# Sigmoid attention and a balanced mixture of experts on one core: quarter-row gathers turned on VectorE for the last two experts, unread products ahead of the first, later places for the routing

## The chip, the core and the metric

The kernel runs on one core of one Trainium2 chip. The metric is device microseconds of one execution; less is better. The engines are TensorE (PE; PEld are its weight loads), VectorE (DVE), ScalarE (ACT), GpSimd (POOL) and SyncE (SP), each with a queue of its own that is worked off in order. DMAs are issued from the queues of SP and POOL.

## What is computed

Inputs: q, k, v of 8 batches, 12 heads, 448 tokens, 64 values each; a gate of 768 x 8; w1 of 8 experts x 768 x 1024, w2 of 8 x 1024 x 768; all float32.

```python
scores = scale * np.matmul(q, k.transpose(0, 1, 3, 2)) - np.log(S)
attn = 1.0 / (1.0 + np.exp(-scores))
x = np.matmul(attn, v)            # then rows of tokens: 3584 x 768
logits = x @ w_gate
order = np.argsort(-logits.flatten())
for idx in order:                 # best pair of token and expert first
    tok, e = (int(idx) // E, int(idx) % E)
    if assigned[tok] >= 0 or counts[e] >= cap:   # cap = 3584 / 8 = 448
        continue
    assigned[tok] = e
    counts[e] += 1
for e in range(E):
    mask = assigned == e
    out[mask] = np.maximum(x[mask] @ w1[e], 0.0) @ w2[e]
```

## The kernel before

**Attention** (lines 484 to 636) runs over 48 pairs of heads and writes the rows x to a DRAM tensor `xs`. The last rows are turned and stored beside the first routing search, up to some 310 us.

**Routing** (`Router.phase`, line 410) finds the experts in eight phases, in the order in which they fill. A phase makes keys (`keys`), turns them on TensorE (line 236), searches a threshold digit by digit on VectorE (`search`; line 281 sets up the digits after the first, line 292 makes the result `kap`), turns that (line 299), and marks the tokens (`pick`, whose last step on VectorE is the column scan of line 326). Then come the *place* (two products, lines 333 and 334), the one-hot tile `r_oh` (line 352), 32 list products (line 360), a copy `r_bt` (line 377), and two products (line 381) that give `r_idx`, the 448 row numbers as four columns of 128. Phase 7 needs no search: `left` takes what remains.

**Experts** (`moe`, line 791) follow one after another, in the program's order, kx = 0 to 7. The first stage has four groups of 36 products per half of w1, 144 x 448 columns in all; after each group ScalarE writes the rectified result as `hb` and `hr` (rounded) and as `h0` (whole; two buffers), and GpSimd writes the remainders from `h0` (line 827). The second stage has two halves of 88 products, 384 columns wide; ScalarE copies the results to `yr` (lines 771 to 783), GpSimd adds one piece (line 784) and scatters the rows to `out` by indirect DMAs (line 757). PSUM has two buffers `sc` for both stages.

**Weights** come in units of 128 x 768, 16 to an expert (8 of w1, 8 of w2, numbered through: expert kx has units 16 kx to 16 kx + 15). A unit is loaded three units ahead (`load_w`) and split two units ahead (`split_w`): ScalarE casts it to `wh`, GpSimd or VectorE subtracts and gives `wl` (line 711). `W_DVE` says which engine: VectorE for units 0 and 1 and for the odd ones from 96.

**Tokens** of the next expert are gathered by four indirect DMAs of whole rows (`gather`, line 731; 128 x 768) and turned in four blocks on TensorE (`xturn`, line 745: two times three transposes a block), from PSUM to `xh` on ScalarE and `xl` on VectorE.

**The order** is written out by hand: `moe` yields after each product with its planned cost (189 or 164 ns), and the driver (line 885) adds these to a clock. When the clock passes `t_route`, the next piece of the routing is emitted, and the T_ numbers set the distance to the piece after; due `chores` (gathers, turning, scatters) are emitted one in 1000 ns, and `flush` empties those that belong to an expert at its end. So the numbers decide where an instruction stands in its queue, and nothing is timed on the chip itself.

Of the kernel before, what the change touches and what calls it, by code (L numbers as in the profile page):

```python
# [54 lines left out]
def route_consts(nc, cp, K):  # L55
# [65 lines left out]
class Router:  # L121
# [217 lines left out]
        nc.vector.tensor_scalar(sl, p[:112, 64:96], BIG, None, OP.add)  # L339
        self.sl = sl  # L340

    def lists(self, alone):

        nc, K, wk, sl = self.nc, self.K, self.wk, self.sl
        P = self.bank()[:112]
# [64 lines left out]
    def phase(self, k):  # L410
        if k:
            self.remove()
        if k < 7:
            if k:
                yield T_KEY
                yield from self.keys()
            yield T_KT if k else T_KEYS
            yield from self.search(k == 0)
            yield T_KAP
            self.pick()  # L420
        else:
            self.left()
        yield T_PICK
        self.place(k == 0)
        yield from self.lists(k == 0)


def moe_attention(tc, q, k, v, w_gate, w1, w2, out):
# [7 lines left out]
    with contextlib.ExitStack() as ctx:  # L436
# [214 lines left out]
        picked, listed = {}, {}  # L651

        def routing():
            for kx in range(E):
                for t in R.phase(kx):
                    if kx not in picked and R.ei is not None:
                        picked[kx] = R.ei
                    yield t
                listed[kx] = R.idx
                R.ei = None  # L660
                yield 0

# [23 lines left out]
        def load_w(u, behind=False):  # L686


            kx, st, i, j = units[u]
            if kx not in gate:  # L690
                gate[kx] = nc.sync.value_load(picked[kx][:1, :1], min_val=0, max_val=E - 1)
            t = wp.tile([128, 768], F32, name="wr")
            if behind:
                nc.gpsimd.memset(t[:1, :1], 0.0)
            if st == 0:
                t = t.rearrange("p (a f) -> p a f", a=3)
                src = w1[ds(gate[kx], 1)].rearrange("e (a p) f -> p (e a) f", p=128)
                nc.sync.dma_start(t, src[:, 3 * j:3 * j + 3, i * 256:(i + 1) * 256])
# [35 lines left out]
        def xturn(kx, j, n, hf, wide):  # L734
# [131 lines left out]
            stream(-1, 2, -1)  # L866
        for j, n in blocks():
            gather(0, j, n)
        stream(-1, 2, 2)
        stream(-1, 4, 2, True)  # L870
        for _ in range(4):
# [13 lines left out]
        for kx in range(E):  # L885
            turned = kx + 1 == E
            start = clock[0]

            def prepare():
                t0 = clock[0]  # L890
                lag = max(5000, min(14000, start + 40000 - t0))
                space = max(TURN_FIRST, min(TURN_NS, (start + EXPERT_NS - t0 - lag - 1000) // 4))
                for j, n in blocks():
                    if kx < 2:
# [4 lines left out]
                def turn_block(j, n):  # L899
# [16 lines left out]
            for step, cost in enumerate(moe(kx)):  # L916
# [12 lines left out]
                    turned = True  # L929
                if turned and kx + 2 in listed and kx + 2 not in fetched:  # L930
                    fetched.add(kx + 2)
                    for j, n in blocks():
                        chores.append((t + 1500 * j, kx + 1, lambda j=j, n=n, e=kx + 2: gather(e, j, n)))
# [39 lines left out]
```

## Time and profile before

| | |
|---|---|
| median of 3 runs | 857.68 us (857.0 to 857.93) |
| profiled execution | 857.27 us, span 855.5 us |
| TensorE busy | 817.9 us, 96% of the span |
| VectorE, ScalarE, GpSimd busy | 538.9, 437.9, 484.4 us |
| attention and first rows | to about 309 us |
| first expert's first product to last product | 325 to 843 us |

The page gives each engine's busy time, the waits say for how long an engine stood idle ahead of an instruction and what ended that, and the timeline lists instructions by their start.

### The profile page before, as it was taken

Reading aid. Unit: us, or ns where it says so; the run is one execution under the profiler, and the core shown is the slowest. Engines: PE = TensorE matmul, PEld = TensorE weight load, DVE = VectorE, ACT = ScalarE, POOL = GpSimd, SP = SyncE. Lnnn points to the kernel's source line nnn. Section 1 sums busy time; section 2 is a strip of 40 time slices with the busy share of each in tenths; the row PEclk is TensorE's granted clock in tenths of the full one; section 3 lists DMA queues with packets and bytes.
Section 4 is the critical chain, followed back from the end, with each engine's and each line's share of the span. In section 5 each row is a group of like instructions: output and inputs, shape, how many; then the busy total and the mean of one; then the engine's idle time right before and its main releaser. Section 6 shows DMA issues by size and latency. Waiting matters only on the chain.

```text
span 855.5 us, 16407 instructions
## 1 busy us (share of the span) xinstructions
PE 817.9 (96%) x5517; PEld 650.2 (76%) x5517; DVE 538.9 (63%) x2069; ACT 437.9 (51%) x603; POOL 484.4 (57%) x506
## 2 busy tenths in 40 slices
PE   6999999999999839999999999999999999999997
PEld 3455455454554728999988999999999989999996
DVE  4565555565554989977978969969879852321211
ACT  6777777778775833425424434434434424443332
POOL 9545444445410014867866866876875885743753
PEclk9999999999999978999999999999999999999999
DMA  9776666656530975345435353453553554443331
GB/s 177 153 153 128 131 129 130 124 118 138 121 65 2 318 254 158 111 138 175 114 106 170 115 147 131 147 169 101 157 166 103 156 156 161 139 129 112 129 103 64
DMA packets 196532, 117.58 MB, mean 137 GB/s; under 512 B 145248, under 2 KB 186208, under 8 KB 196448
## 3 DMA queue, kind: packets, MB, share of 16 engines
q1 hardware_dynamic: 183840, 83.30, 37.6%
q0 software_dynamic: 10752, 33.02, 12.6%
q8 instruction: 43, 0.70, 0.4%
q10 hardware_dynamic: 1856, 0.23, 0.2%
q14 instruction: 41, 0.34, 0.1%
HBM read 94.47 MB, written 22.02 MB: 136 GB/s over the span
## 4 chain that ended last, share of the span: by engine, by line
PE 85%; DVE 10%; issue 2%; DMA 1%; ACT 0%; POOL 0%; ACTq 0%; POOLq 0%; SPq 0%; DVEq 0%
PE sc L856 26%; PE tp L559 13%; PE sc L535 12%; PE sc L811 8%; PE sc L815 8%; PE sc L813 8%; DVE r_junk L178 4%; PE tp L565 3%; PE tp L745 2%; PE sc L545 2%; PE tp L580 1%; PE rt L360 1%; DVE r_j L272 1%; DVE r_T L281 1%; DMA xr<-xs,r_idx 1%
## 5 line engine op out<-in xcount | busy, mean ns | idle before, releaser
L711 POOL TENSOR_TENSOR wl<-wr,wh 128x768 fp32r<-128x768 f32 x110 | 202.3, 1855 | 28.3 <-ACT wh L709 28.0
L856 PE MATMUL sc<-wh,hb 128*128 128x384 f32 x768 | 199.8, 338 | 0.0
L525 ACT ACTIVATE at<-sc,bias 128x896 f32<-128x896 f32 x168 | 160.8, 1004 | 62.2 <-PE sc L545 37.8
L466 POOL DMA_DIRECT2D nkq<-in_q_dram x188 | 118.2, 640 | 114.5 <-DVE kqT L510 109.3
L813 PE MATMUL sc<-xl,wh 128*128 128x448 f32 (+2 forms) x396 | 144.2, 364 | 0.0
L811 PE MATMUL sc<-xh,wh 128*128 128x448 f32 (+2 forms) x396 | 144.2, 364 | 0.0
L815 PE MATMUL sc<-xh,wl 128*128 128x448 f32 (+2 forms) x396 | 143.9, 363 | 0.0
L856 PEld LDWEIGHTS sc<-wh,hb 128*128 128x128 f32 x768 | 138.3, 188 | 1.7 <-issue 0.6
L856 PE MATMUL sc<-wl,hb 128*128 128x384 f32 x384 | 130.8, 341 | 0.0
L709 ACT ACTIVATE wh<-wr 128x768 fp32r<-128x768 f32 x128 | 104.0, 850 | 50.9 <-PE sc L856 29.9
L178 DVE TENSOR_SCALAR_CACHE_REDUCE r_junk<-r_KE,r_T 128x224 bf16<-128x224 f32 x315 | 123.3, 442 | 0.1
L559 PE MATMUL tp<-at,nv 128*64 128x448 f32 x576 | 118.6, 548 | 0.0
L821 ACT ACTIVATE hb<-sc 128x768 fp32r<-128x768 f32 x32 | 26.0, 813 | 134.0 <-PE sc L815 134.0
L519 DVE TENSOR_TENSOR kqL<-kqT,kqH 128x896 fp32r<-128x896 f32 (+1 forms) x49 | 52.5, 1072 | 57.8 <-ACT kqH L517 57.7
L827 POOL TENSOR_TENSOR hb<-h,hb 128x768 fp32r<-128x768 f32 x32 | 59.1, 1848 | 50.4 <-ACT h L824 50.4
L559 PEld LDWEIGHTS tp<-at,nv 128*64 128x64 f32 x576 | 37.1, 136 | 59.4 <-issue 57.1
L813 PEld LDWEIGHTS sc<-xl,wh 128*128 128x128 f32 x396 | 74.6, 188 | 6.9 <-DVE xl L749 0.2
L815 PEld LDWEIGHTS sc<-xh,wl 128*128 128x128 f32 x396 | 74.6, 188 | 6.8 <-issue 0.2
L811 PEld LDWEIGHTS sc<-xh,wh 128*128 128x128 f32 x396 | 74.6, 188 | 6.6
L711 DVE TENSOR_TENSOR wl<-wr,wh 128x768 fp32r<-128x768 f32 x18 | 24.0, 1332 | 82.1 <-ACT wh L709 82.0
L856 PEld LDWEIGHTS sc<-wl,hb 128*128 128x128 f32 x384 | 72.2, 188 | 1.8 <-issue 1.0
L535 PE MATMUL sc<-kqH 64*128 64x448 f32 x288 | 59.8, 412 | 6.9 <-ACT kqH L517 6.9
(185 smaller groups left out, 1232.8 us busy)
## 6 DMA issues: line engine op xcount, KB each, us to landing
wr<-in_moe_w_dram SPq DMA_DIRECT2D x128, 384.0 KB, 3.3
xs<-xr SPq DMA_DIRECT2D x32, 336.0 KB, 4.7
nkq<-in_k_dram SPq DMA_DIRECT2D x190, 56.0 KB, 2.5
nkq<-in_q_dram POOLq DMA_DIRECT2D x188, 56.0 KB, 2.6
nv<-in_v_dram SPq DMA_DIRECT2D x94, 96.0 KB, 2.5
nr<-in_v_dram SPq DMA_DIRECT2D x48, 32.0 KB, 2.2
xr<-xs,r_idx POOLq DMA_INDIRECT x32, 4.6
out_dram<-yr,r_idx POOLq DMA_INDIRECT x32, 3.6
```

Of the source, the lines that this page charges most:

```text
L178: nc.vector.tensor_scalar(junk[:, a:b], self.KE[:, a:b], T[:, i:i + 1].bitcast(F32), None, OP.is_ge, OP.add, accum_out=cnt[:, i:i + 1])
L466: qn.dma_start(t[o:o + 32, n], rws[x])
L525: nc.scalar.activation(a, p[:, :, :S], AF.Sigmoid, bias=bias, scale=1 / math.sqrt(D))
L535: nc.tensor.matmul(p[:, j, :S], R[half, c * 128:(c + 1) * 128], M[half], start=i == 0, stop=i == 2)
L559: nc.tensor.matmul(p[j * 64:j * 64 + 64, :S], nat["v", b, g][:, h0 + j, c, :], AT[b, pr, c][:, j, :], start=(c == 0), stop=(c == 2 and pr ...
L709: nc.scalar.activation(hi, raw[u], AF.Copy)
L711: eng.tensor_tensor(lo, raw[u], hi.bitcast(F32), OP.subtract)
L811: nc.tensor.matmul(ph[:, f, lo:hi], wh[:, a, fs], xh[:, dd, lo:hi], start=st, stop=False)
L813: nc.tensor.matmul(ph[:, f, lo:hi], wh[:, a, fs], xl[:, dd, lo:hi], start=False, stop=False)
L815: nc.tensor.matmul(ph[:, f, lo:hi], wl[:, a, fs], xh[:, dd, lo:hi], start=False, stop=en)
L827: nc.gpsimd.tensor_tensor(h2, h0[:, :, t], h1.bitcast(F32), OP.subtract)
L856: nc.tensor.matmul(o, hs, w[:, a], start=st and n == 0, stop=en and n == len(terms) - 1)
```

## The change

- For experts 6 and 7 (`BY_DVE = 6`) the rows are gathered in quarters: `xs` is seen as 4 x 3584 rows of 192 values, and partition group g of a tile gets quarter g of 32 tokens. Each expert takes 14 indirect DMAs of 128 x 192 (`gather_quarters`) in place of four of 128 x 768. Then 32 x 32 blocks turned by VectorE (`vturn`) give what TensorE's transposes gave, in another order of the 768 values; w1 of these experts is loaded in that order, by four DMAs of 32 partitions in place of one.
- `lists` makes the quarter numbers `r_idq` with eight more products for each of these experts.
- Splits of all units from 91 on are VectorE's (before: of the odd ones from 96).
- `FILL = 6` products of 128 x 224 stand on TensorE between the first expert's gathers and its first transposes; nobody reads them.
- `T_PICK` goes from 2800 to 3000, the last phase has `T_LEFT = 3500`, and a turned row block of expert 0's time holds the routing's clock back by 1100 instead of 600.

```diff
-T_KEYS, T_KE, T_STEP, T_KAP, T_PICK, T_TOT, T_OH, T_BT = 3600, 2100, 2050, 500, 2800, 600, 3800, 600
+T_KEYS, T_KE, T_STEP, T_KAP, T_PICK, T_TOT, T_OH, T_BT = 3600, 2100, 2050, 500, 3000, 600, 3800, 600
+T_LEFT = 3500
+FILL = 6
+TURN_E1 = 1100
+BY_DVE = 6
+FETCH = {6: (0, 1000), 7: (18000, 2500)}
+VTURN = {6: (7000, 3800), 7: (31000, 3000)}
-W_DVE = 96
+W_DVE = lambda u: u >= 91
...
+        if quarters:
+            for u in range(2):
+                for g in range(4):
+                    nc.tensor.matmul(p[32 * g:32 * g + 32, 8 + 8 * u:16 + 8 * u], bt[:, 32 * u:32 * u + 32], K.SELG,
+                                     start=True, stop=True)
...
+            self.idq = wk.tile([128, 8, 2], I32, name="r_idq")
+            nc.vector.tensor_scalar(self.idq, p[:, 8:24].rearrange("p (u s) -> p s u", u=2), 4.0, K.gq, OP.mult, OP.add)
...
-        yield T_PICK
+        yield T_PICK if k < 7 else T_LEFT
...
+                    src = w1[ds(gate[kx], 1)].rearrange("e (g a p) f -> g p (e a) f", g=4, a=ND)
+                    for g in range(4):
+                        nc.sync.dma_start(t[32 * g:32 * g + 32], src[g, :, 3 * j:3 * j + 3, fs])
...
-            eng = nc.vector if u < 2 or (u >= W_DVE and u % 2) else nc.gpsimd
+            eng = nc.vector if u < 2 or W_DVE(u) else nc.gpsimd
...
+        def gather_quarters(kx, s):
+            j, i = s // 4, s % 4
+            if i == 0:
+                xg[kx, j] = xp.tile([128, DM], F32, name="xr", bufs=XR_BUFS)
+            nc.gpsimd.indirect_dma_start(out=xg[kx, j][:, 192 * i:192 * i + 192], out_offset=None,
+                                         in_=xs.rearrange("t (g w) -> (t g) w", g=4),
+                                         in_offset=bass.IndirectOffsetOnAxis(ap=quarter[kx][:, s // 2, s % 2:s % 2 + 1], axis=0))
+
+        def vturn(kx, j, n, hf):
...
+            p = ps_t.tile([128, 512], F32, name="tp")
+            v = xg[kx, j].rearrange("p (i w) -> p i w", w=192)[:, :n // 32, 96 * hf:96 * hf + 96]
+            nc.vector.transpose(p[:, :3 * n].rearrange("p (a i w) -> p a i w", a=3, w=32),
+                                v.rearrange("p i (a w) -> p a i w", w=32))
+            pv = p[:, :3 * n].rearrange("p (a t) -> p a t", a=3)
+            sl = (slice(None), slice(hf * 3, hf * 3 + 3), slice(j * 128, j * 128 + n))
+            nc.scalar.activation(xh[sl], pv, AF.Copy)
+            return lambda: nc.vector.tensor_tensor(xl[sl], pv, xh[sl].bitcast(F32), OP.subtract)
...
+        for _ in range(FILL):
+            nc.tensor.matmul(p[:, 0, :224], ident, R.KE, start=True, stop=True)
...
+            def fetch(e, t, due):
+                if e >= BY_DVE:
+                    for s in range(S // 32):
+                        chores.append((t + FETCH[e][0] + FETCH[e][1] * s, due, lambda s=s: gather_quarters(e, s)))
...
+                    for j, n in blocks():
+                        chores.append((t0 + VTURN[kx + 1][0] + VTURN[kx + 1][1] * j, kx + 1,
+                                       lambda j=j, n=n: vturn_block(kx + 1, j, n)))
+                    return
...
-                    turning["used"] += TURN_DVE
+                    turning["used"] += TURN_DVE if kx else TURN_E1
```

Three places in the queues. GpSimd at the border of experts 5 and 6, before (`L757` scatters, `L784` is the yr addition, `L711` a split, `L827` the remainders of expert 6's first group):

```order
L756 MEMSET spacer 1x1
L757 DMA out_dram<-yr,r_idx 3584x768
L784 TENSOR_TENSOR yr<-yr,rest 64x384
L711 TENSOR_TENSOR wl<-wr,wh 128x768
L756 MEMSET spacer 1x1
L757 DMA out_dram<-yr,r_idx 3584x768
L756 MEMSET spacer 1x1
L757 DMA out_dram<-yr,r_idx 3584x768
L756 MEMSET spacer 1x1
L757 DMA out_dram<-yr,r_idx 3584x768
L827 TENSOR_TENSOR hb<-h_10090,hb 128x2x384
L827 TENSOR_TENSOR hr<-h_10090,hr 128x2x64
```

The same place in the changed kernel, whose lines are numbered anew (`L814` scatters, `L841` is the yr addition, `L786` a quarter-row gather, `L884` the remainders):

```order
L813 MEMSET spacer 1x1
L814 DMA out_dram<-yr,r_idx 3584x768
L841 TENSOR_TENSOR yr<-yr,rest 64x384
L786 DMA xr<-xs,r_idq 128x192 x14
L813 MEMSET spacer 1x1
L814 DMA out_dram<-yr,r_idx 3584x768
L813 MEMSET spacer 1x1
L814 DMA out_dram<-yr,r_idx 3584x768
L813 MEMSET spacer 1x1
L814 DMA out_dram<-yr,r_idx 3584x768
L884 TENSOR_TENSOR hb<-h_10145,hb 128x2x384
L884 TENSOR_TENSOR hr<-h_10145,hr 128x2x64
```

The 14 gathers of expert 7 stand in one run, between the yr addition and three scatters, and the split is gone.

VectorE around the last place, before (from the scan of phase 7 to its row numbers):

```order
L326 SCALAR_TENSOR_TENSOR r_tot<-r_mk 112x64
L408 CAST r_ei<-csum 1x1
L336 SCALAR_TENSOR_TENSOR r_nm<-r_mk,rt 112x64
L337 TENSOR_REDUCE rt<-r_nm 112x32
L339 TENSOR_SCALAR r_sl<-rt 112x32
L348 TENSOR_SCALAR rt<-r_sl 112x32
L350 SCALAR_TENSOR_TENSOR rt<-rt,r_sl 112x32
L364 TENSOR_TENSOR rt<-rt,c_io_963 112x256
L365 TENSOR_TENSOR c_mv<-rt,c_tok 112x256
L352 TENSOR_TENSOR r_oh<-c_io_963,rt 112x2048
L377 CAST r_bt<-rt 128x64
L383 TENSOR_SCALAR r_idx<-rt 128x4
```

In the changed kernel (`L742` is a split):

```order
L342 SCALAR_TENSOR_TENSOR r_tot<-r_mk 112x64
L432 CAST r_ei<-csum 1x1
L742 TENSOR_TENSOR wl<-wr,wh 128x768
L352 SCALAR_TENSOR_TENSOR r_nm<-r_mk,rt 112x64
L353 TENSOR_REDUCE rt<-r_nm 112x32
L355 TENSOR_SCALAR r_sl<-rt 112x32
L364 TENSOR_TENSOR rt<-r_sl 112x32
L366 SCALAR_TENSOR_TENSOR rt<-rt,r_sl 112x32
L380 TENSOR_TENSOR rt<-rt,c_io_1052 112x256
L381 TENSOR_TENSOR c_mv<-rt,c_tok 112x256
L368 TENSOR_TENSOR r_oh<-c_io_1052,rt 112x2048
L742 TENSOR_TENSOR wl<-wr,wh 128x768 x2
```

One split stands ahead of the place and two behind the one-hot tile, ahead of the copy `r_bt`.

ScalarE in the second half of expert 5's second stage, before (`L709` weight casts, `L748` casts of turned tokens, `L771` and `L774` yr copies):

```order
L748 ACTIVATE xh<-tp 128x3x128 x2
L709 ACTIVATE wh<-wr 128x768
L748 ACTIVATE xh<-tp 128x3x128 x2
L709 ACTIVATE wh<-wr 128x768
L748 ACTIVATE xh<-tp 128x3x64 x2
L709 ACTIVATE wh<-wr 128x768
L771 COPY yr<-sc 128x2x384
L774 COPY yr<-sc 128x384
```

In the changed kernel (`L740`, `L801`, `L828` and `L831` in the same roles):

```order
L740 ACTIVATE wh<-wr 128x768 x2
L801 ACTIVATE xh<-tp 128x3x128 x6
L740 ACTIVATE wh<-wr 128x768
L801 ACTIVATE xh<-tp 128x3x64 x2
L740 ACTIVATE wh<-wr 128x768
L828 COPY yr<-sc 128x2x384
L831 COPY yr<-sc 128x384
```

Three blocks' casts now stand together, and the last block's are the third instruction pair ahead of the copy that frees a PSUM buffer.

## Rows read from the trace of the kernel before

**Rows 1.** Head of the page: span, and busy time of each engine with its share and instructions.
```profile
span 855.5 us, 16407 instructions
PE 817.9 (96%) x5517; PEld 650.2 (76%) x5517; DVE 538.9 (63%) x2069; ACT 437.9 (51%) x603; POOL 484.4 (57%) x506
```

**Rows 2.** Waits of TensorE from 325 to 845 us: who waited for whom, us in total, times, longest.
```profile
PE rt L299 <- DVE r_kap L292: 1.7, 1, 1.7
PE tp L745 <- DMA xr<-xs,r_idx: 0.9, 1, 0.9
PE sc L745 <- DVE xl L749: 0.6, 1, 0.6
PE rt L334 <- DVE r_ei L320: 0.4, 1, 0.4
PE rt L334 <- DVE r_ei L408: 0.3, 1, 0.3
```

**Rows 3.** Timeline of TensorE: start, duration (which reaches into the next instruction's), line, operation, tiles, shapes, count. A full block and the short block of turning between products, and the 32 list products.
```profile
707.41 0.82 PE L745 MATMUL tp<-ident,xr 128*128 128x128 f32 x6
707.99 0.42 PE L856 MATMUL sc<-wh,hb 128*128 128x384 f32 x1
708.25 0.34 PE L856 MATMUL sc<-wl,hb 128*128 128x384 f32 x1
...
753.98 0.58 PE L745 MATMUL tp<-ident,xr 64*128 64x64 f32 x6
754.49 0.47 PE L811 MATMUL sc<-xh,wh 128*128 128x448 f32 x1
754.80 0.36 PE L813 MATMUL sc<-xl,wh 128*128 128x448 f32 x1
...
441.65 1.18 PE L360 MATMUL rt<-r_oh,c_mv 112*32 112x64 f16 x32
```

**Rows 4.** Groups by line: count, then busy us and mean ns of one, then the engine's idle time ahead of them.
```profile
L510 DVE STREAM_TRANSPOSE kqT<-nkq 128x896 f32<-128x896 f32 x47 | 51.9, 1105 | 3.2 <-DMA nkq<-in_k_dram 1.8 <-DMA nkq<-in_q_dram 0.4 <-DMA nv<-in_v_dram 0.2
L648 POOL DMA_INDIRECT xr<-in_moe_w_gate_dram,c_t x1 | 1.0, 1002 | 32.3 <-PE tp L565 32.3
L827 POOL TENSOR_TENSOR hb<-h,hb 128x768 fp32r<-128x768 f32 x32 | 59.1, 1848 | 50.4 <-ACT h L824 50.4
L827 POOL TENSOR_TENSOR hr<-h,hr 128x128 fp32r<-128x128 f32 x32 | 19.1, 597 | 0.0
L709 ACT ACTIVATE wh<-wr 128x768 fp32r<-128x768 f32 x128 | 104.0, 850 | 50.9 <-PE sc L856 29.9
```

**Rows 5.** Timeline of GpSimd and of VectorE at the first expert's gathers.
```profile
317.06 1.71 POOL L731 DMA_INDIRECT xr<-xs,r_idx  x1 [42.61 <-DMA wr<-in_moe_w_dram]
319.07 0.97 POOL L731 DMA_INDIRECT xr<-xs,r_idx  x1 [0.30 <-issue]
320.34 0.95 POOL L731 DMA_INDIRECT xr<-xs,r_idx  x1 [0.30 <-issue]
...
316.94 0.96 DVE L711 TENSOR_TENSOR wl<-wr,wh 128x768 fp32r<-128x768 f32 x1 [0.67 <-ACT wh L709]
318.24 0.96 DVE L711 TENSOR_TENSOR wl<-wr,wh 128x768 fp32r<-128x768 f32 x1 [0.35 <-ACT wh L709]
```

**Rows 6.** Timeline at the start of expert 6: its first product, GpSimd's yr addition, and ScalarE's cast after the fourth group of its first stage.
```profile
726.08 0.36 PE L811 MATMUL sc<-xh,wh 128*128 128x448 f32 x1
727.82 1.01 POOL L784 TENSOR_TENSOR yr<-yr,rest 64x384 f32<-64x384 f32 x1 [1.18 <-ACT yr L783]
758.50 0.81 ACT L821 ACTIVATE hb<-sc 128x768 fp32r<-128x768 f32 x1 [2.81 <-PE sc L815]
```

**Rows 7.** Timeline of expert 1's time: TensorE, VectorE and GpSimd at the third search, its list and the gather.
```profile
433.71 0.32 PE L299 MATMUL rt<-ident,r_kap 128*112 128x128 f32 x1 [1.67 <-DVE r_kap L292]
450.51 0.88 PE L745 MATMUL tp<-ident,xr 128*128 128x128 f32 x6 [0.89 <-DMA xr<-xs,r_idx]
...
395.70 2.79 DVE L281 TENSOR_SCALAR r_T<-c_kk,r_J 128x3 int32<-128x3 int32 x1
...
396.62 1.83 POOL L711 TENSOR_TENSOR wl<-wr,wh 128x768 fp32r<-128x768 f32 x1
445.88 0.99 POOL L731 DMA_INDIRECT xr<-xs,r_idx  x1 [0.16 <-issue]
```

**Rows 8.** Timeline of expert 5's time: the column scan of phase 7 on VectorE, and GpSimd's remainder and two splits.
```profile
692.90 1.39 DVE L326 TENSOR_TENSOR_SCAN r_tot<-r_mk 112x64 bf16<-112x64 bf16 x1
...
692.29 1.84 POOL L827 TENSOR_TENSOR hb<-h,hb 128x768 fp32r<-128x768 f32 x1 [0.32 <-ACT h L824]
685.62 3.67 POOL L711 TENSOR_TENSOR wl<-wr,wh 128x768 fp32r<-128x768 f32 x2
```

**Rows 9.** The start of the first expert. [...]
```profile
309.00:315.50 6.50, 1.80 (x34) 1.31 (x34) 5.20 (x20) 0.00 (x0) 0.00 (x0) 0.50 0.76 252
326.00:329.50 3.50, 3.50 (x31) 3.50 (x31) 3.19 (x17) 1.27 (x3) 0.34 (x1) 0.99 0.91 317
...
322.28 0.88 PE L745 MATMUL tp<-ident,xr 128*128 128x128 f32 x3 [6.22 <-issue]
325.64 0.56 PE L813 MATMUL sc<-xl,wh 128*128 128x256 f32 x1
...
325.03 0.56 DVE L749 TENSOR_TENSOR xl<-tp,xh 128x384 fp32r<-128x384 f32 x1
```

More of the change, by code (lines that the diff above doesn't have):

```diff
@@ L104, in route_consts @@
     nc.vector.tensor_scalar(K.SEL, t6, t7, None, OP.is_equal)
+    t11 = cp.tile([128, 8], I32, name="c_t11")
+    nc.gpsimd.iota(t11, [[1, 8]], base=0, channel_multiplier=0)
+    t12 = cp.tile([128, 1], I32, name="c_t12")
+    nc.gpsimd.iota(t12, [[0, 1]], base=32 * 7168, channel_multiplier=1)
+    K.SELG = cp.tile([128, 8], F16, name="c_SELG")
+    nc.vector.tensor_scalar(K.SELG, t11, t7, None, OP.is_equal)
+    nc.vector.tensor_scalar(t12, t12, 5, None, OP.logical_shift_right)
+    K.gq = cp.tile([128, 1], F32, name="c_gq")
+    nc.vector.tensor_copy(K.gq, t12)
+    yield
     K.kk = cp.tile([128, 16, 3], I32, name="c_kk")
@@ L340, in place, with lists @@
         self.sl = sl
-    def lists(self, alone):
+    def lists(self, alone, quarters):
         nc, K, wk, sl = self.nc, self.K, self.wk, self.sl
@@ L422, in phase @@
             self.left()
-        yield T_PICK
+        yield T_PICK if k < 7 else T_LEFT
         self.place(k == 0)
-        yield from self.lists(k == 0)
+        yield from self.lists(k == 0, k >= BY_DVE)
 def moe_attention(tc, q, k, v, w_gate, w1, w2, out):
@@ L650, in moe_attention @@
         late.pop(0)()
-        picked, listed = {}, {}
+        picked, listed, quarter = {}, {}, {}
         def routing():
@@ L659, in routing @@
                 listed[kx] = R.idx
+                quarter[kx] = getattr(R, "idq", None)
                 R.ei = None
@@ L696, in load_w @@
                 t = t.rearrange("p (a f) -> p a f", a=3)
-                src = w1[ds(gate[kx], 1)].rearrange("e (a p) f -> p (e a) f", p=128)
-                nc.sync.dma_start(t, src[:, 3 * j:3 * j + 3, i * 256:(i + 1) * 256])
+                fs = slice(i * 256, (i + 1) * 256)
+                if kx < BY_DVE:
+                    src = w1[ds(gate[kx], 1)].rearrange("e (a p) f -> p (e a) f", p=128)
+                    nc.sync.dma_start(t, src[:, 3 * j:3 * j + 3, fs])
+                else:
+                    src = w1[ds(gate[kx], 1)].rearrange("e (g a p) f -> g p (e a) f", g=4, a=ND)
+                    for g in range(4):
+                        nc.sync.dma_start(t[32 * g:32 * g + 32], src[g, :, 3 * j:3 * j + 3, fs])
             else:
@@ L749, in xturn, with vturn_block @@
             nc.vector.tensor_tensor(xl[sl], pv, xh[sl].bitcast(F32), OP.subtract)
+        def gather_quarters(kx, s):
[6 more added lines that the diff above has]
+        def vturn(kx, j, n, hf):
+            if (j, hf) == (0, 0):
+                XH[kx] = (xp.tile([128, ND, S], F32R, name="xh", bufs=2),
+                          xp.tile([128, ND, S], F32R, name="xl", bufs=2))
+            xh, xl = XH[kx]
+            p = ps_t.tile([128, 512], F32, name="tp")
[6 more added lines that the diff above has]
+            return lambda: nc.vector.tensor_tensor(xl[sl], pv, xh[sl].bitcast(F32), OP.subtract)
+        def vturn_block(kx, j, n):
+            for rest in [vturn(kx, j, n, hf) for hf in range(2)]:
+                rest()
         scat, chores = [], []
@@ L887, in moe_attention @@
             start = clock[0]
+            def fetch(e, t, due):
+                if e >= BY_DVE:
+                    for s in range(S // 32):
+                        chores.append((t + FETCH[e][0] + FETCH[e][1] * s, due, lambda s=s: gather_quarters(e, s)))
+                else:
+                    for j, n in blocks():
+                        chores.append((t + 1500 * j, due, lambda j=j, n=n: gather(e, j, n)))
             def prepare():
@@ L891, in prepare @@
                 lag = max(5000, min(14000, start + 40000 - t0))
+                if kx + 1 >= BY_DVE:
+                    if kx + 1 not in fetched:
+                        fetch(kx + 1, t0, kx + 1)
+                    for j, n in blocks():
+                        chores.append((t0 + VTURN[kx + 1][0] + VTURN[kx + 1][1] * j, kx + 1,
+                                       lambda j=j, n=n: vturn_block(kx + 1, j, n)))
+                    return
                 space = max(TURN_FIRST, min(TURN_NS, (start + EXPERT_NS - t0 - lag - 1000) // 4))
@@ L931, in moe_attention @@
                     fetched.add(kx + 2)
-                    for j, n in blocks():
-                        chores.append((t + 1500 * j, kx + 1, lambda j=j, n=n, e=kx + 2: gather(e, j, n)))
+                    fetch(kx + 2, t, kx + 1)
                 if t >= t_chore:
```

2 lines of the change are left out of this document (added).

## The prediction

> **What bounds the kernel now.** The page's head comes first: TensorE is busy 817.9 us of a span of 855.5 [rows 1]. The profiled execution took 857.27 us, 1.77 outside its span and 0.41 below the median of 857.68; I make the sum against the profiled execution and add its difference to the median. Next come TensorE's waits from 325 to 845 us, all eight experts: five, together 3.9 us [rows 2]. So there TensorE's own queue is the clock: an instruction taken from it shortens the run by its place in that queue, one put into it lengthens the run, and work on other engines costs only where TensorE comes to wait for it. Last I read the rows around each place that the change moves. E is the start of expert 6 (numbers from 0), 726.08 us in the trace [rows 6]; a first-stage product holds 0.207 us of the queue, a second-stage one 0.175.
>
> **The change, part by part.**
>
> (a) *Turning off TensorE.* Six transposes stood between two products that start 0.17 apart otherwise: 707.41 to 707.99, and the next start 0.26 later, so a full block costs 0.58 + 0.26 - 0.175 = 0.66; the short block 0.51 + 0.31 - 0.207 = 0.61 [rows 3]. Two experts: 2 x (3 x 0.66 + 0.61) = 5.2 us saved. Nothing else lies under them, so this is the surest term (5.1 to 5.3).
>
> (b) *Sixteen small list products* (eight for each of the last two lists) on TensorE. 32 products of the list step take 1.1 us of the queue [rows 3], 0.034 each, so +0.6 (0.3 to 1.0; 128x32 weights each are not in the trace).
>
> (c) *The routing's clock, expert 1.* TensorE waits 1.67 us for the third search's result at 433.71 [rows 7]. That search cannot start earlier or later with TensorE: its first-digit instruction at 395.70 lasts 2.79 for 128 x 3 values, until GpSimd's subtraction from 396.62 ends [rows 7]. The changed order puts 6 products more ahead of the waiting transpose (2 at place 1, 3 ahead of the key transposes, 1 after), 6 x 0.175 = 1.05 us of work for the wait, so 0.62 is left. Behind it TensorE waits 0.89 us at 450.51 for the gather of 445.88, which stood behind GpSimd's yr addition and a subtraction; those follow the half's end, now 1.05 earlier, while the transposes come 0.35 later (two more products). That wait goes. -1.9 in all; bounds -0.2 (the search moves along after all: one product) and -2.6 (both waits gone).
>
> (d) *Places.* A column scan on VectorE that meets a GpSimd operation ends with it: 692.90 lasts 1.39, as long as the hb subtraction of 692.29 [rows 8]. The larger T_PICK gives 2 x 0.175 more at each place, but the places move against GpSimd. By counting products, the scan of list 6 falls at 686.0 of the old trace, into the subtractions from 685.62 (two, 1.83 each) [rows 8]: it ends at 687.6, where its product is due at 687.15, +0.5. List 5 in the same way +0.5, lists 3 and 4 +0.1 each, and list 7, with a weight split ahead of its place and two ahead of its copy, +0.3. The two old waits of 0.4 and 0.3 [rows 2] go. Net +0.8; bounds -0.7 (no scan collides) and +4 (lists 5 and 6 lose a second GpSimd operation each).
>
> (e) *The six unread products.* TensorE's clock is at 0.50 from 309 us to 326 [rows 9]; the fills run in the 6.2 us in which it waits for the first gather, so they cost nothing: a transpose of 128 columns takes at most 0.29 at half clock (three in 0.88 at 322.28), so six products of 224 columns take 3.1, and 6.1 if one takes twice as long, a bound. If the clock then stays up, the gain is small, because VectorE's third xl (325.03, 0.56) releases the second product at 325.64 [rows 9], and VectorE is busy with keys until 323.6: 0.2 there and 0.2 on products up to 326.0. I take -0.2, between 0 and -0.5.
>
> (f) *Start of expert 6.* Its gathers wait for list 6; ten run early, the last four stand behind the yr addition of expert 5's first half. That ends 2.75 us after the half (as 727.82 + 1.01 against E [rows 6]); four gathers at 1.27, one pair of splits in the way (0.74, below), and 4.63 from issue to use (445.88 to 450.51): the last lands 11.9 us after the half. On VectorE the third block then takes about 2.2 (two transposes of 0.47, from 1105 ns for 896 columns [rows 4], and ScalarE and two subtractions), a split 0.96, the short block 1.2: 13.8. Behind its copies ScalarE has a weight cast (0.85) and the yr copy that frees the PSUM bank for expert 6 (0.8): 15.5, against 88 products x 0.175 = 15.4. I take +0.5; 0 to 3, the transposes being unmeasured.
>
> (g) *The burst.* The 14 gathers of expert 7 were given 18 us of delay, but the flush at expert 5's end empties them all at once: they stand in a row ahead of three scatters and of every hb subtraction of expert 6. How long GpSimd takes does not hang on row size: 1002 ns for 32-byte rows and 0.95 to 0.97 for 3072-byte ones [rows 4, 5]; one starts 1.27 after another. So: yr addition until E + 2.75, 14 x 1.27 = 17.8, three scatters at 1.3, the first hb and hr 1.85 + 0.60 [rows 4]: E + 26.9. h0 has two buffers, so ScalarE's third h0, due at E + 23.4 (108 products x 0.207 and the two hb casts), waits for that; then h0 1.0, the cast of unit 104 0.85, its split 0.96: E + 29.7. TensorE wants unit 104 at 758.50 - 726.08 - 2.6 (turning) = E + 29.8 [rows 6]. Without any disturbance it just holds. But all splits are on VectorE now, six of them during the burst, and a gather that met two of them took 1.71 instead of 0.97 [rows 5]: three pairs, 3 x 0.74 = 2.2 more, so TensorE waits about 2.1. Bounds 0 and 5.7 (every split adds its whole 0.96).
>
> Behind this wait TensorE alone is late; ScalarE's later casts follow with time to spare. The other edits cost nothing: the quartered w1 loads (64 instead of 16 issues) are asked for three units ahead, some 11 us, and no wait of TensorE is for weights [rows 2]; if that cover went, each late unit would show as a wait of its own. GpSimd loses 21 splits of 1.83 [rows 8], VectorE gains them at 0.96 [rows 5] as its searches end.
>
> Sum: -5.2 + 0.6 - 1.9 + 0.8 - 0.2 + 0.5 + 2.1 = -3.3 us: 854.0 for a profiled execution, **854.4 us** for the median.
>
> **Rivals.**
> *The burst is covered* (0.23). Gathers lose nothing to splits, no scan collides: -5.2 + 0.6 - 1.9 - 0.2 - 0.2 = -6.9, 850.8 us. For it: undisturbed, (g) closes to 0.1 us. Against: each of the three pairs must fall between gathers.
> *A split shuts GpSimd out for its whole length* (0.17). Six splits add 6 x 0.96 = 5.8 to the burst; (g) becomes 5.7: 858.0 us, no change that can be measured. For it: the wait at 395.70 was the whole of the other operation [rows 7]. Against: the gather of 317.06 grew by 0.74, not by the 1.92 of both splits. [...]
> *Slower: a quarter-row gather costs more than a whole-row one* (0.12). Fourteen of them decide (g), four decide (f): 18 x excess. The gain is eaten at 3.3/18 = 0.18 over 1.27, a spacing of 1.45; at 1.7 the time is 857.68 - 3.3 + 7.7 = 862.1. For it: no row has this form, and 1.71 occurs. Against: 32-byte rows cost the same.
> *The unread products and the clock settings do nothing* (0.06): without (c) and (e), 856.5.
>
> **How the numbers follow.** The forecast holds 0.42, from 852.5 to 856.3 by itself. About 0.2% (1.7 us) is what a measurement of this kernel can tell from no change: faster means under 856.0, slower over 859.4. Faster: nearly all of the forecast, the covered burst, a little of the rest, 0.66; same 0.20; slower 0.14. For 8 in 10 the range reaches to the covered burst and past the lock: 850.5 to 859.0.
>
> **What would show it.** (a): no transposes after expert 5's start, 2.6 us fewer in each of the last two experts. (c): waits of about 0.6 and 0 at the third search and its gather. (d): waits of about 0.5 at the places of lists 5 and 6. (e): a clock at 1.00 when the first transposes run. (f), (g): waits at E and at unit 104, the first product of expert 6's second stage, there with ScalarE idle ahead of the third h0 until GpSimd's first hr is done. Wrong it would be if the gathers come closer than 1.27 or further apart than 1.45, if VectorE's transposes into PSUM take over a microsecond, or if a wait for weights appears.

## The result and the profile after

The changed kernel took **863.22 us** (median of 4; 862.91 to 863.73) against 857.47 beside it: ratio 1.0064, 95% interval 1.0052 to 1.0077. It is slower by 0.64%, and 4.2 us above my range. Run again beside the experiments it took 863.62 and 862.38 on two occasions and 856.59 (0.9977, 0.9966 to 0.9988) on another; the kernel before stayed at 857.4 to 857.6 on these. The 856.59 is a median of eight executions of which one was slow (1016.73); without that one it is 856.27. The section on the experiments shows what differs in the traces; why it differs stays open.

The page's head, against [rows 1]: TensorE is busy longer though 48 transposes are gone.

```profile
span 861.4 us, 16622 instructions
PE 821.2 (95%) x5497; PEld 650.2 (75%) x5497; DVE 568.4 (66%) x2111; ACT 438.4 (51%) x603; POOL 468.8 (54%) x507
```

TensorE's waits from 325 to 845 us, against [rows 2]:

```profile
PE sc L872 <- issue: 2.5, 2, 1.7
PE tp L776 <- DMA xr<-xs,r_idx: 1.9, 1, 1.9
PE sc L868 <- issue: 1.3, 2, 1.1
PE rt L350 <- DVE r_ei L336: 1.2, 2, 0.7
PE sc L872 <- DVE wl L742: 0.9, 1, 0.9
...
PE rt L315 <- DVE r_kap L308: 0.6, 1, 0.6
PE sc L870 <- issue: 0.5, 2, 0.4
```

The wait for `kap` is 0.6 where it was 1.7, and a new one for a gather has come. The three lines on `issue` (L868, L870, L872 are the three products of the first stage) are waits that no instruction ends; they had no like before. Taking each expert from its first product to the next one's in TensorE's timeline, in the recorded execution and in one of the occasion with 856.59 (occasion 5 below), each minus before:

| stretch | predicted | recorded | occasion 5 |
|---|---|---|---|
| up to expert 0's end (e) | -0.2 | -0.1 | +0.7 |
| expert 1 (c) | -1.9 | -2.1 | -2.1 |
| experts 2 to 4 (d) | +0.3 | +2.2 | +1.7 |
| expert 5 (half of a, b, d, f) | -1.0 | -1.9 | -2.1 |
| expert 6 (half of a, g) | -0.5 | +7.2 | +1.3 |
| expert 7 and the end | 0 | +0.6 | +0.6 |
| sum | -3.3 | +5.9 | +0.2 |

So three stretches are dearer than predicted: expert 6 with the burst (g), experts 2 to 4, and the end. Expert 5 is cheaper, by 0.9 and 1.1. The burst's place, in the recorded execution; E is 724.17 here. First stretches (busy us of PE, PEld, DVE, ACT, POOL, granted clock, DMA share, GB/s), then the timeline of TensorE, ScalarE and GpSimd:

```profile
735.00:743.70 8.70, 8.70 (x43) 7.89 (x43) 1.29 (x2) 0.16 (x1) 6.87 (x7) 1.00 0.56 169
743.70:752.00 8.30, 3.92 (x13) 2.68 (x12) 0.00 (x0) 1.47 (x3) 6.34 (x10) 0.77 0.43 143
752.00:760.00 8.00, 7.12 (x23) 5.53 (x22) 6.68 (x4) 4.92 (x8) 6.42 (x4) 0.60 0.37 103
```

```profile
738.95 0.37 PE L872 MATMUL sc<-xh,wl 128*128 128x448 f32 x1
...
743.70 0.37 PE L870 MATMUL sc<-xl,wh 128*128 128x448 f32 x1
744.86 0.37 PE L872 MATMUL sc<-xh,wl 128*128 128x448 f32 x1 [0.79 <-issue]
...
745.47 0.37 PE L872 MATMUL sc<-xh,wl 128*128 128x448 f32 x1
746.99 0.36 PE L868 MATMUL sc<-xh,wh 128*128 128x448 f32 x1 [1.15 <-issue]
747.72 0.36 PE L870 MATMUL sc<-xl,wh 128*128 128x448 f32 x1 [0.36 <-issue]
749.82 0.53 PE L872 MATMUL sc<-xh,wl 128*128 128x448 f32 x1 [1.74 <-issue]
...
733.57 1.59 ACT L740 ACTIVATE wh<-wr 128x768 fp32r<-128x768 f32 x2
750.53 0.81 ACT L878 ACTIVATE hb<-sc 128x768 fp32r<-128x768 f32 x1 [15.37 <-remote]
...
726.79 1.51 POOL L786 DMA_INDIRECT xr<-xs,r_idq  x1 [0.16 <-issue]
...
734.86 1.38 POOL L786 DMA_INDIRECT xr<-xs,r_idq  x1 [0.30 <-issue]
...
744.04 0.95 POOL L786 DMA_INDIRECT xr<-xs,r_idq  x1 [0.30 <-issue]
...
748.80 1.82 POOL L884 TENSOR_TENSOR hb<-h,hb 128x768 fp32r<-128x768 f32 x1
750.56 0.47 POOL L884 TENSOR_TENSOR hr<-h,hr 128x128 fp32r<-128x128 f32 x1
```

ScalarE's second `hb` waits for the product of 738.95 and starts at 750.53, 11.2 us after that product's end. In the program it waits for TensorE alone, not for GpSimd, and the buffer that it writes was last read in expert 5; the trace calls the signal that released it `remote`, one that it can give to no instruction. From 743.9 on TensorE stands between single products of one group, none of which waits for another engine. I call the two together the *standstill*. It ends at about 751, just after the last packet of the scatters behind the gathers (750.4 in the trace). From 752 to 760 the clock is at 0.60 on average.

### The profile page after: what moved, and what is told of

It is laid out like the page before. It is cut to its first block, busy times and chain, and to the rows that moved or that the text cites. A ratio compares the mean times of both kernels' runs of the same rounds, so it can differ in the third digit from the quotient of the medians.

```text
span 861.4 us, 16622 instructions
## 1 busy us (share of the span) xinstructions
PE 821.2 (95%) x5497; PEld 650.2 (75%) x5497; DVE 568.4 (66%) x2111; ACT 438.4 (51%) x603; POOL 468.8 (54%) x507
## 4 chain that ended last, share of the span: by engine, by line
PE 79%; DVE 11%; SPq 2%; DMA 2%; another core or an unknown queue 2%; issue 2%; ACT 1%; POOL 0%; POOLq 0%; ACTq 0%; DVEq 0%
PE sc L913 25%; PE tp L583 13%; PE sc L559 10%; PE sc L868 7%; PE sc L872 7%; PE sc L870 7%; DVE r_junk L194 4%; PE tp L589 2%; PE sc L569 2%; PE tp L776 1%; PE tp L604 1%; SPq L490 1%; DMA wr<-in_moe_w_dram 1%; PE rt L376 1%
## 5 line engine op out<-in xcount | busy, mean ns | idle before, releaser
L742 POOL TENSOR_TENSOR wl<-wr,wh 128x768 fp32r<-128x768 f32 x89 | 162.4, 1844 | 23.7 <-ACT wh L740 23.3
L872 PE MATMUL sc<-xh,wl 128*128 128x448 f32 (+2 forms) x396 | 144.9, 366 | 3.4 <-issue 2.5
L868 PE MATMUL sc<-xh,wh 128*128 128x448 f32 (+2 forms) x396 | 145.3, 367 | 2.1 <-issue 1.3
L870 PE MATMUL sc<-xl,wh 128*128 128x448 f32 (+2 forms) x396 | 144.8, 366 | 0.5 <-issue 0.5
L740 ACT ACTIVATE wh<-wr 128x768 fp32r<-128x768 f32 x128 | 103.6, 850 | 49.7 <-PE sc L913 20.1
L742 DVE TENSOR_TENSOR wl<-wr,wh 128x768 fp32r<-128x768 f32 x39 | 47.0, 1234 | 80.4 <-ACT wh L740 75.7
L884 POOL TENSOR_TENSOR hb<-h,hb 128x768 fp32r<-128x768 f32 x32 | 59.7, 1867 | 56.0 <-ACT h L881 56.0
L868 PEld LDWEIGHTS sc<-xh,wh 128*128 128x128 f32 x396 | 75.2, 190 | 11.3 <-issue 2.8
L872 PEld LDWEIGHTS sc<-xh,wl 128*128 128x128 f32 x396 | 75.2, 190 | 10.7 <-issue 2.4
L870 PEld LDWEIGHTS sc<-xl,wh 128*128 128x128 f32 x396 | 75.3, 190 | 7.9 <-issue 0.9
```

The source lines that it names most:

```text
L868: nc.tensor.matmul(ph[:, f, lo:hi], wh[:, a, fs], xh[:, dd, lo:hi], start=st, stop=False)
L870: nc.tensor.matmul(ph[:, f, lo:hi], wh[:, a, fs], xl[:, dd, lo:hi], start=False, stop=False)
L872: nc.tensor.matmul(ph[:, f, lo:hi], wl[:, a, fs], xh[:, dd, lo:hi], start=False, stop=en)
L884: nc.gpsimd.tensor_tensor(h2, h0[:, :, t], h1.bitcast(F32), OP.subtract)
```

## The experiments

An occasion is one set of kernels on one chip, with its own runs of the kernel before. Medians in us:

| kernel | recorded | 1 | 2 | 3 | 4 | 5 | 6 |
|---|---|---|---|---|---|---|---|
| before | 857.47 | 857.38 | 857.51 | 857.57 | 857.66 | 857.38 | 858.05 |
| changed | 863.22 | | 863.62 | 862.38 | | 856.59 | |
| changed, w1 whole | | 855.71 | | 863.26 | | | |
| gathers spaced | | 852.21 | | 852.85 | | | |
| spaced, w1 whole | | | 853.55 | | | | |
| half the run | | | | | 853.56 | | |
| subtractions instead | | 859.40 | | | 859.88 | 859.68 | 861.09 |
| three h0 buffers | | | | | 856.48 | 856.61 | |
| settings alone | | 857.13 | | | | | |
| spaced, other gathers 1000 ns | | | 854.76 | | | | |
| spaced, expert 3's 1000 ns | | | | | 852.21 | | |

**The run of gathers.** The 14 gathers of expert 7 keep their own times:

```diff
-                    fetch(kx + 2, t, kx + 1)
+                    fetch(kx + 2, t, kx + 1 + (kx + 2 == 7))
```

> The changed kernel, but the 14 quarter gathers of expert 7 are no longer emptied in one run at the end of expert 5: they keep their own times (2.5 us apart), so on GpSimd they stand between the scatters and the remainders of expert 6. The changed kernel lost 9.8 us in the first stage of expert 6 (its expert 6 took 69.99 us, the one of before 62.80 with 2.6 us of turning in it). Theory A (the run of gathers is the cause, by whatever it blocks): the 9.8 us vanish, 853 to 854 us. Theory B (the fourfold w1 loads are the cause): the loss stays, 862 to 864 us. Theory C (VectorE's splits and turning are the cause): the loss stays or halves, 858 to 864 us.

852.21 us, ratio 0.9939 (0.9922 to 0.9955); expert 6 took 60.35 us instead of 69.99, with no wait of TensorE in it. So the fourfold loads, the splits and the turning, which are all still there, do not make the loss without the run of gathers. The changed kernel was not run on this occasion; beside it, on occasion 3:

> The kernel with the spaced gathers once more, as the base of the two: both theories 851.5 to 853 us, and expert 6 in 60.2 to 60.5 us.

852.85 (0.995; 0.9934 to 0.9967) against the changed kernel's 862.38, expert 6 in 59.89 against 69.34. The run of gathers is the cause of the loss; what in it costs the time is asked below.

**The fourfold loads.**

```diff
-                if kx < BY_DVE:
+                if kx < E:
                     src = w1[ds(gate[kx], 1)].rearrange("e (a p) f -> p (e a) f", p=128)
```

> The changed kernel with w1 of experts 6 and 7 loaded whole, one DMA a unit as before instead of four of 32 partitions; w1 then stands in the wrong order of the 768 values, so the products of these two experts are not the right ones, but their number and times are. Theory A (the run of gathers): the 9.8 us of expert 6 stay, 862.5 to 864 us. Theory B (four times as many loads, with their semaphores): they vanish, 853 to 855 us.

855.71, between the two theories: no standstill, one wait of 2.50 at unit 104. That looked like theory B, but the changed kernel had not run beside it. So:

> The changed kernel once more, unchanged, beside the others on one chip. In its first execution TensorE stood still for single products of expert 6 between 743.9 and 751.2 us with no wait that the kernel names, and ScalarE's second hb of that expert started at 750.53, 11.2 us after its products. The kernel that keeps the run of gathers but loads w1 whole showed neither (855.7 us, on another occasion). Theory P (the fourfold loads together with the run of gathers do it): 862.5 to 864 us here too, with the same standstill. Theory Q (it belonged to that occasion, not to the program): 855 to 857 us, with one wait of about 2.5 us at unit 104 in place of the standstill.

> The changed kernel, beside the two that follow on one chip, because the 855.7 us of the kernel with whole w1 loads and the 863 us of the changed one were never taken on the same occasion. Theory P (run of gathers and fourfold loads together): 862 to 864 us. Theory Q (the standstill of TensorE and ScalarE belongs to occasions, whatever the loads): the same as the kernel with whole loads, within 1.5 us, be it 856 or 863.

> The kernel with the run of gathers and whole w1 loads once more (products of experts 6 and 7 not the right ones). Theory P: 855 to 857 us, 6 to 8 us below the changed kernel beside it, with a wait of TensorE of about 2.5 us at unit 104 and no standstill. Theory Q: within 1.5 us of the changed kernel, and with the same standstill of TensorE and ScalarE if that one has it.

863.62; then 862.38 and, beside it, 863.26 for the whole loads, both profiles with the standstill. Theory Q holds: the loads are not it. Within an occasion it need not come every time either: of the ten executions with whole loads (857.8 to 864.9) three lie under 860, but their traces are not kept. Without the run of gathers the loads cost nothing:

> As the kernel with the spaced gathers, with w1 of experts 6 and 7 loaded whole (their products are then not the right ones; number and times are). My prediction put the fourfold loads at nothing. If that holds: 852 us, the same within 0.8. If the loads cost by themselves: 848 to 850.5 us.

853.55, 0.7 and 1.3 above the spaced kernel of the two other occasions. The second is more than the 0.8 that I allowed, but the wrong way for a cost of the loads: none can be seen.

**Lateness or transfers.** On the kernel with the spaced gathers, at the end of expert 5:

```diff
             flush(kx + 1)
+            if kx + 1 == 6:
+                for _ in range(18):
+                    nc.gpsimd.tensor_tensor(R.KE, R.KE, R.KE, OP.subtract)
```

> As the kernel with the spaced gathers, but GpSimd gets 18 subtractions of 128 x 224 values (some 0.78 us each by the rows of hb and hr, 14 us, nobody reads them) where the run of gathers stood, so that its first remainder of expert 6 is as late as in the changed kernel, without transfers. Theory A1 (only GpSimd's lateness counts: ScalarE waits for it, TensorE for ScalarE): some 9 us slower than the kernel with the spaced gathers, 861 to 864 us. Theory A2 (the transfers themselves hold up TensorE's and ScalarE's signals): only the 0 to 3 us of my term (g), 853 to 857 us.

859.40, 7.2 above the spaced kernel, so A2 falls: GpSimd's lateness alone is dear, without standstill. A1's 861 to 864 is not reached either. Spaced gathers stand between the late remainders here, so ScalarE's `h0` waits for GpSimd twice and TensorE for ScalarE. TensorE's waits from 724 to 795 us, in the same kernel's execution on occasion 5:

```profile
PE sc L913 <- ACT h L881: 2.7, 1, 2.7
PE sc L913 <- ACT yr L828: 1.4, 1, 1.4
```

Whether the standstill needs the transfers was asked three times more:

> The kernel with 18 unread subtractions in place of the run of gathers once more (859.4 us on the first occasion, two waits of TensorE of 2.69 and 1.44, and half clock behind them). Theory T (the standstill comes from the transfers): again 858 to 860 us, and ScalarE's second hb of expert 6 starts within 0.2 us of its products' end. Theory L (it comes from GpSimd's lateness): 862 to 865 us, with ScalarE's second hb some 10 us late.

> 18 unread subtractions in place of the run of gathers. Theory T (the transfers make the standstill): 858.5 to 860.5 us and no standstill, also where the changed kernel has one. Theory L (GpSimd's lateness makes it): 2 to 6 us above that where the changed kernel stands still.

> 18 unread subtractions in place of the run of gathers, a fourth time. Theory T (the transfers make the standstill): 858.5 to 860.5 us on any occasion, ScalarE's second hb of expert 6 within 0.2 us of its products. Theory L (GpSimd's lateness makes it), if this is an occasion of the slow sort: 861.5 to 866 us with ScalarE's second hb some 10 us late. If it is one of the other sort the run tells nothing new.

859.88, 859.68 and 861.09, never a standstill in the profiles. But the changed kernel beside the second had none either, and nothing shows that the other two fell on an occasion that has it, so T against L stays open. Two more on the size of the run and on what it holds up:

```diff
-   chores.append((t + FETCH[e][0] + FETCH[e][1] * s, due, lambda s=s: gather_quarters(e, s)))
+   chores.append((t + FETCH[e][0] + FETCH[e][1] * s, due if e < 7 or s < 7 else e, lambda s=s: gather_quarters(e, s)))
```

> The changed kernel, but only seven of the 14 gathers of expert 7 are emptied in one run; the other seven keep their times. By the arithmetic of my term (g), GpSimd's first hr of expert 6 is done at E + 18 and ScalarE's third h0 is due at E + 23.4: no wait, 852 to 853 us, under theory L and the plain queue alike. If a shorter run of transfers holds the signals up as well (theory T, in proportion): 4 to 5 us lost, 856 to 858 us.

853.56, half a microsecond above the forecast; GpSimd's first `hr` of expert 6 is done at E + 18.1 (forecast E + 18), and TensorE waits nowhere in that expert. For a short run (g) is right about when GpSimd is through.

```diff
-                    h0 = hp.tile([128, 2, S], F32, name="h0", bufs=2)
+                    h0 = hp.tile([128, 2, S], F32, name="h0", bufs=3)
```

> The changed kernel with the whole run of gathers, and three buffers for h0 instead of two. GpSimd is as late, but ScalarE's third h0 of expert 6 no longer waits for it. Plain queue (my term (g)): the wait at unit 104 goes; what is left is the wait of the second stage for the late remainders, 853 to 856 us. Theory T: the standstill stays, ScalarE's second hb again 10 us late, 861 to 864 us.

> The run of gathers with three buffers for h0. Theory T: the same standstill as the changed kernel beside it (861 to 864 us where that one has it, 855 to 857 where not). Theory L: 855 to 857.5 us either way, since ScalarE never waits for GpSimd there.

856.48 and 856.61, the second beside

> The changed kernel, beside the two that follow. With a standstill: 861.5 to 864 us, ScalarE's second hb of expert 6 some 10 us behind its products. Without one: 855 to 857 us, as the kernel with whole loads (855.7), with one wait of TensorE of about 2.5 us ahead of the second stage of expert 6. Which of the two it is, no theory says.

which gave 856.59: where nothing stands still, a third buffer changes nothing in the median. The changed kernel in that execution (E is 724.31), timeline of TensorE, ScalarE, GpSimd and VectorE:

```profile
753.56 0.51 PE L913 MATMUL sc<-wh,hb 128*128 128x384 f32 x2
756.55 0.44 PE L913 MATMUL sc<-wl,hb 128*128 128x384 f32 x1 [2.48 <-DVE wl L742]
...
751.73 0.92 ACT L881 ACTIVATE h<-sc 128x896 f32<-128x896 f32 x1 [4.29 <-POOL hr L884]
752.54 1.57 ACT L740 ACTIVATE wh<-wr 128x768 fp32r<-128x768 f32 x2
...
742.78 1.58 POOL L786 DMA_INDIRECT xr<-xs,r_idq  x1 [0.30 <-issue]
...
751.24 0.46 POOL L884 TENSOR_TENSOR hr<-h,hr 128x128 fp32r<-128x128 f32 x1
751.65 1.84 POOL L884 TENSOR_TENSOR hb<-h,hb 128x768 fp32r<-128x768 f32 x1
753.46 0.45 POOL L884 TENSOR_TENSOR hr<-h,hr 128x128 fp32r<-128x128 f32 x1
753.88 1.79 POOL L884 TENSOR_TENSOR hb<-h,hb 128x768 fp32r<-128x768 f32 x1
755.64 1.16 POOL L884 TENSOR_TENSOR hr<-h,hr 128x128 fp32r<-128x128 f32 x1
...
753.41 3.08 DVE L742 TENSOR_TENSOR wl<-wr,wh 128x768 fp32r<-128x768 f32 x1 [9.87 <-ACT wh L740]
```

and its stretches around the wait:

```profile
754.00:757.00 3.00, 0.52 (x3) 0.45 (x3) 3.00 (x2) 3.00 (x6) 3.00 (x3) 1.00 0.00 0
757.00:761.50 4.50, 4.50 (x18) 4.50 (x18) 4.50 (x4) 0.25 (x1) 2.74 (x2) 0.62 0.49 123
```

The links of my chain are there: the third `h0` waits for GpSimd's first `hr`, then the cast, then VectorE's split of unit 104, then TensorE. Their sizes are not mine. The split starts at E + 29.1 and TensorE wants it at E + 29.8, so a split of 0.96 would have left a wait of 0.3; it takes 3.08, and only this makes the wait 2.48. Behind the wait the clock is at 0.62 on average: 18 products of 0.175 in 4.5 us, 1.35 lost. With three buffers ScalarE is on time, and TensorE waits 2.48 and 1.41 in the two executions profiled for the split alone. These two executions are the shortest of their ten (853.44 and 855.00), with expert 6 in 62.55 and 61.95; what the others lost, whose medians equal the one with two buffers, is not in the traces kept. VectorE's split and TensorE's wait, then GpSimd's remainders beside it, at three buffers (occasion 4):

```profile
746.58 7.49 DVE L742 TENSOR_TENSOR wl<-wr,wh 128x768 fp32r<-128x768 f32 x1 [5.46 <-ACT wh L740]
...
754.12 0.44 PE L913 MATMUL sc<-wl,hb 128*128 128x384 f32 x1 [2.48 <-DVE wl L742]
...
746.08 0.91 POOL L814 DMA_INDIRECT out_dram<-yr,r_idx  x1 [0.22 <-issue]
747.01 1.86 POOL L884 TENSOR_TENSOR hb<-h,hb 128x768 fp32r<-128x768 f32 x1
748.82 0.46 POOL L884 TENSOR_TENSOR hr<-h,hr 128x128 fp32r<-128x128 f32 x1
749.24 1.83 POOL L884 TENSOR_TENSOR hb<-h,hb 128x768 fp32r<-128x768 f32 x1
...
753.22 1.16 POOL L884 TENSOR_TENSOR hr<-h,hr 128x128 fp32r<-128x128 f32 x1
```

The late remainders follow each other without a gap. The split starts during the last scatter, 0.43 before the first of them, and ends at 754.07, when five are through and the sixth, of 1.16 instead of 0.46, is running. The splits of [rows 5] take 0.96; this one, of 7.49, had started before all of these and yet was not through before five of them were. What holds it, no row shows.

**The settings.** `BY_DVE = 8` and the splits as before leave the routing's clock and the unread products:

> The changed kernel without its VectorE turning, quarter gathers and splits (BY_DVE 8, W_DVE as before): only the settings of the routing's clock and the six unread products are left. My theory from the trace of the changed kernel: expert 1 ends 2.1 us earlier, and a gather wait of 1.9 us in expert 2 gives it back; 857.2 to 857.7 us, no change. Rival (the wait in expert 2 comes from something else that the change moved): 855.3 to 856 us, faster.

857.13, ratio 1.0003 (0.9991 to 1.0015): nothing. Expert 1 is 2.1 shorter, expert 2 is 1.6 longer. GpSimd at the gathers for expert 3 in the changed kernel, and TensorE's transposes that wait for the second:

```profile
507.04 0.98 POOL L762 DMA_INDIRECT xr<-xs,r_idx  x1 [5.85 <-DVE rt L415]
509.55 1.01 POOL L841 TENSOR_TENSOR yr<-yr,rest 64x384 f32<-64x384 f32 x1 [1.52 <-ACT yr L840]
510.53 1.84 POOL L742 TENSOR_TENSOR wl<-wr,wh 128x768 fp32r<-128x768 f32 x1
512.52 0.98 POOL L762 DMA_INDIRECT xr<-xs,r_idx  x1 [0.16 <-issue]
...
517.50 0.74 PE L776 MATMUL tp<-ident,xr 128*128 128x128 f32 x5 [1.88 <-DMA xr<-xs,r_idx]
```

In the kernel before the second gather stood right behind the first, at 508.78, ahead of the yr addition of 511.56. The two rows of before:

```profile
508.78 0.96 POOL L731 DMA_INDIRECT xr<-xs,r_idx  x1 [0.30 <-issue]
511.56 1.01 POOL L784 TENSOR_TENSOR yr<-yr,rest 64x384 f32<-64x384 f32 x1 [1.82 <-ACT yr L783]
```

To put it back, the gathers of experts 3 to 5 were handed out 1000 ns apart, and then those of expert 3 alone (both on the spaced kernel; the diff shows the second, and one of its two like lines):

```diff
-   chores.append((t + 1500 * j, due, lambda j=j, n=n: gather(e, j, n)))
+   chores.append((t + (1000 if e == 3 else 1500) * j, due, lambda j=j, n=n: gather(e, j, n)))
...
```

> As the kernel with the spaced gathers, but the whole-row gathers of experts 3 to 5 are handed out 1000 ns of the clock apart instead of 1500. On GpSimd the second gather for expert 3 then stands ahead of the yr addition and a split instead of behind them (in the kernel before it ran at 508.78, in the changed one behind the addition, and TensorE waited 1.7 to 1.9 us for it). My theory: that wait goes, 1.5 to 1.8 us faster than the kernel with the spaced gathers, 850.3 to 850.8 us. Rival (the transposes then wait for the third gather, or the split behind it comes too late): no gain, 852 us.

> The kernel with the spaced gathers, with the gathers of expert 3 alone 1000 ns apart (those of experts 4 and 5 at 1500 as before). The second one then stands ahead of the yr addition and a split on GpSimd. My theory: the wait of 1.2 to 1.9 us of expert 2 goes and no other takes its place: 850.3 to 851.3 us, the fastest so far. Rival (the earlier end of expert 2 meets GpSimd elsewhere, as it did when all three experts' gathers were moved: waits of 1.0 and 1.5 us in expert 3): 852 to 854 us.

854.76 and 852.21: no gain, as the rivals had it, and the first is a loss. The wait goes and expert 2 is 2 us shorter (66.1), but expert 3 is 1.7 to 2.7 longer (67.2 and 68.2; 65.5 in the spaced kernel): its place comes to wait 0.9 instead, and one of its turned blocks 0.3 or 1.5. Such a wait is passed on, not removed. The fastest kernel stays the one with the spaced gathers, 0.5 to 0.6% under before.

## Why the prediction was wrong, point by point

- **(a) right.** Beside the kernel with the settings alone, the spaced one has expert 5 2.5 us shorter (67.59 to 65.05) and expert 6 2.5 (62.86 to 60.35): 5.0 with (b), the last two places and (f) in it, against -5.2 for (a) alone. A pair of VectorE's transposes into PSUM takes 1.05 us, 0.11 more than I took from [rows 4].
- **(b), (f) smaller than predicted.** Eight of the new list products hold TensorE's queue for 0.14 us (694.40 to the next product at 694.54), 0.3 for both lists against 0.6. At E nothing waits in the recorded execution, and 0.20 in one other.
- **(c) right in its place, wrong in the sum.** The wait for `kap` is 0.65 (forecast 0.62), the one for the gather 0, expert 1 2.1 shorter (1.9). I looked no further than the stretch in which it is won: the settings put the second gather for expert 3 behind other work of GpSimd, 1.9 back (0.8 to 1.8 in the other profiles of this order). That it is T_PICK and not the holding back by turned blocks is not shown; the two were not run apart.
- **(d) near in the sum, not place by place.** TensorE waits 0.52 at the place of list 6 (forecast 0.5). At list 3 the old wait of 0.44 did not go but became 0.69 (forecast 0.1). At list 7 the old 0.3 went and no new wait came (0.3); at list 5 there is none in the recorded execution (0.5), and 1.04 in two of the other profiles. Together +0.5 against +0.8.
- **(e) right in the clock, not shown in the gain.** The transposes run at clock 1.00 from 322.1. But the stretch up to expert 0's end differs from before by -1.2 to +1.3 over the profiles taken (and by +3.3 in one), and no run leaves out the unread products alone, so a gain of 0.2 cannot be told from none.
- **(g) the step that failed: the price of the burst.** The row of gathers is where I put it, at 1.25 from one to the next where no split meets it (I took 1.27). The chain behind it has the right links, but two of its terms are wrong. The splits lengthened the gathers by 1.0 in the recorded execution (1.51 and 1.38 instead of 0.95) and by 1.2 on occasion 5 (1.51 and 1.58; one pair of splits of three cost nothing), not by 2.2, so GpSimd's first `hr` was done at E + 26.9 and E + 27.4 and not at the E + 29.1 that my terms add up to. And the split of unit 104, taken at 0.96, lasted 3.08 beside GpSimd's remainders, which stand in a row while it catches up. The one error is 1.7 too dear and the other 2.1 too cheap: that TensorE waits 2.48 where I said 2.1 is luck. The lower clock behind the wait, 0.62 on average, costs 1.35 and had no term. So where nothing stands still the burst costs 64.08 - 60.35 = 3.7 instead of 2.1 (4.1 on occasion 1, with whole loads). On three of the occasions, the recorded one among them, the standstill came on top: 69.99 - 60.35 = 9.6, beyond the 5.7 that I gave as bound. No term of mine had it, and its cause stays open.
- **The end** is 0.84 longer from the last product on in every profile with quarter gathers, and not longer with the settings alone. I had nothing for it; it lies behind the start of the last scatter (5.75 from there to the end of the span instead of 4.90), and is not explained.
- **The rivals.** "The burst is covered" is false, though the gathers lost only about half of what I took. "A split shuts GpSimd out", the lock that the range speaks of, had the right pair of engines and the wrong victim: the gathers that met a pair of splits took 1.38 to 1.58 instead of 0.95, not the 1.92 more of both, while the split of unit 104 lasted 3.08 and 7.49 instead of 0.96. No run shows such a lock as a rule. Gathers do not cost more a quarter (0.95, 1.25 from one to the next); that its 862.1 is near the 863.2 is luck. "The unread products and the clock settings do nothing" is right in the sum (857.13 against 857.38) and not in the reason: 2.1 is won in expert 1 and 1.6 lost in expert 2.

What stays open is the standstill. It came only in kernels with the whole run of 14 gathers and three scatters, and only on the recorded occasion and on 2 and 3; the spaced kernels on 2 and 3 had none. In its four profiles ScalarE's late `hb` starts 0.1 to 1.3 us after the last packet of the run, yet on occasions 1, 4 and 5 the same run held up neither TensorE's signals nor ScalarE. It does not go with the chip: occasions 1 and 3 were on the same one. On the three occasions that have it the profiles also lack records of signals (TensorE's instructions give 576, the trace of the changed kernel has 552, of the spaced one 561), on the others none is missing. That the two have to do with each other is not shown.

## What to carry to other kernels

Work that is given a late due time can still be emptied all at once by the flush that ends its stage: look at the order for long runs of one kind on a queue, and price not only when the queue is through but what stands behind it without a gap then, and whom that keeps waiting. An instruction moved to win a wait has to be followed into the next stage; here that happened twice, each time one expert later. And a time that an occasion can change by 6 us is worth a second occasion before a cause is named: the whole loads looked like the cause until they ran beside the changed kernel.

## What was not expected of the hardware

A VectorE split of 0.96 us lasted 7.49 beside back-to-back subtractions of GpSimd. A wait of TensorE of 2.5 us was followed by a stretch of 4.5 us in which the granted clock was 0.62 on average, with 18 products in it; with three buffers the products behind a wait as long stood 0.17 apart (14 from 754.40 to 756.83). On some occasions an instruction of ScalarE that waits for TensorE alone began 11 to 12 us after the product's end (11.2 in the recorded execution).
